# Padded loads, a reordered opening, GpSimd triangles and unit-matrix products in a chunked linear-attention kernel with a feed-forward block

## The chip, the cores and the metric

The kernel runs on one core of one Trainium2 chip. The metric is device time in microseconds (us) of the whole program. Before the change the median of three timed runs is 633.68 us (632.99 to 636.66).

## The reference

Two stages, in float32. A recurrent attention over 768 steps with a state of 40 x 40 for each of 4 batches and 8 heads (32 independent systems), and then a feed-forward block on its output, with 320 channels (8 heads of 40) and 1280 hidden ones.

```python
# B, H, S, D = 4, 8, 768, 40
for t in range(S):
    kt, vt, rt = (k[:, :, t], v[:, :, t], r[:, :, t])
    wt, at, bt = (w[:, :, t], a[:, :, t], b[:, :, t])
    y[:, :, t] = np.einsum('bhd,bhde->bhe', rt, state)
    Sa = np.einsum('bhde,bhe->bhd', state, at)
    state_decay = state * wt[:, :, None, :] - np.einsum('bhd,bhe->bhde', Sa, bt)
    state = state_decay + np.einsum('bhd,bhe->bhde', vt, kt)
...
x = y.transpose(0, 2, 1, 3).reshape(B, S, H * D)
xn = (x - mu) / np.sqrt(var + 1e-06) * g_ln
out = x + np.maximum(xn @ w_ch1, 0.0) @ w_ch2
```

The inputs arrive as host arrays that were laid out beforehand: `ea` holds w and a of a chunk, `eb` k and b, `rd` and `vr` r and v by rows of the 40 channels, `vt` v by steps. The two weight matrices arrive as float64 and are turned into float32 on the chip.

## The kernel before, in words

**Chunks.** The 768 steps are cut into 24 chunks of 32, and the recurrence inside a chunk is solved in closed form with products of small matrices; two chunks make a slab. The 32 systems lie in two halves of 16, one at partition rows 0 to 39, one at 64 to 103, so a tile of "104 rows" holds both.

**One chunk** passes these steps, each a function of the code.

- `prep` loads `wa` (from `ea`) and `bk` (from `eb`). VectorE forms running products of w with scans: `gE` (L335), its reciprocal `last` (L337), and `qE` backwards (L339). `aT` = a * qE (L343) and `bk` *= gE (L351), on VectorE for chunks below `EARLY` = 4 and on GpSimd from there. A transfer puts aT into the block tile `abd`. TensorE forms the gram products (L361, bank<-abd,bk), VectorE evacuates them with a mask of signs into `gk` (L364), and transfers store gk to DRAM (`d_l`, the triangles; `d_k`, the part for the products with x).
- `invert`, once a slab: the triangles of both chunks come back from DRAM into `yv` (64 partitions, one system of one chunk each), and 14 steps of two VectorE instructions (L403 into ytmp, L407 into yv) invert their diagonal blocks; a ScalarE copy (L409) and two stores (`d_h`) follow.
- `merge`: four loads of `hv` from d_h, two TensorE products (L428, L439) and two ScalarE copies (`qm`, `tt`) make the full inverse of a chunk.
- `loads`: transfers into the operand tiles (`x2s`, `x5s`, `vu`), and transposes of bk by TensorE (L464).
- `chain` is the recurrence proper: the product L487, its negated copy `hn` (ScalarE), the product with the inverse (L497, bank<-hn,tt), four ScalarE copies into x (L501), the state update (L514) and its VectorE evacuation with the decay (L521).
- `post` makes the output of a chunk: transposes of u (L535) and of the state (ScalarE copies behind them), `rbd` loaded from `rd`, a product `z` masked into `x5s` by VectorE (L573), the product y and its evacuation `xt` (L588).
- `norm` and `moe`: layer norm of xt and its transposes; for every two chunks ten blocks of the hidden layer, each with eight up products (L753), ScalarE `hh`, VectorE `hl` (L758, the low part of a two-part split) and six down products (L737).

**The weights.** `weights` loads them after the mark ("go",), which is chunk 0's qE scan, and converts them in 22 quarters through three buffers (`ot_0`, `ot_1`, `m`). A quarter is: ScalarE Abs, VectorE's shift (L626) and merge of the low word (L627), then the sign. For some quarters the sign is VectorE's third pass (L630); for ten quarters of w2 (`sel`) ScalarE makes a Sign and GpSimd multiplies by it (L634). Behind it stand the scaling and the high copy, and a residue `w` = m - high on GpSimd (L670), after which the buffer is free.

**The order.** All of this is entered as tasks into a planner (`Plan`) with an engine, an estimated duration, a key (a due time in chunks) and what the task reads and writes. `Plan.order` is a list scheduler: it gives each engine the ready task that can start first and, among those, the one of the lowest key, with its estimates alone. The result is one fixed row of instructions for TensorE, VectorE, ScalarE, GpSimd and for SyncE, which issues all transfers in order. For a transfer the planner assumes kb/200 us on the pipe. ("first",) marks the task behind which the transfers of chunks 2 and 3 may go.

Of the kernel before, what the change touches and what calls it, by code (L numbers as in the profile page):

```python
# [11 lines left out]
F32 = mybir.dt.float32  # L12
# [8 lines left out]
NCH = 24  # L21
# [11 lines left out]
ROWS = [slice(r, r + D) for r in HROW]  # L33
QUADS = [slice(32 * q, 32 * q + 32) for q in range(4)]
SLAB = 2
NSLAB = NCH // SLAB
EARLY = 4
# [12 lines left out]
class Plan:  # L50
# [4 lines left out]
    READ, FETCH, STALL = 128, 3.6, 0.2  # L55

# [28 lines left out]
    def order(self, free):  # L85
# [31 lines left out]
        while len(out) < len(T):  # L117
# [41 lines left out]
            if t["eng"] == "SP":  # L159
                pipe = max(pipe, end + 1.3) + t["kb"] / 200.0  # L160
                done = pipe + 0.7 + t["late"]
# [13 lines left out]
        return out  # L175


@with_exitstack
def body(ctx, tc, ea, eb, vr, rd, vt, w1, w1x_in, w2, gl, fe, fd, out):
# [35 lines left out]
    gk, = ring(1, "gk", 512)  # L215
# [31 lines left out]
    two = lambda x, i, n=2: [(x, i, y) for y in range(n)]  # L247

# [72 lines left out]
    def prep(c):  # L321
        i, s, j, k = c % 2, c // SLAB, c % SLAB, c % BK
        kp = c - 3.4
# [3 lines left out]
        after = [("first",)] if 2 <= c < 4 else []  # L327
        kl = kp + (0.5 if 2 <= c < 4 else -1.0 if c < 2 else 0.0)
        for hf in (1, 0):
            dma(kl - 1.3, 167, after, [W[hf]], t[ROWS[hf]], ea[c, hf])  # L330
        for hf in (1, 0):
            dma(kl - 1.1, 164, after, [K[hf]], tb[ROWS[hf]], eb[c, hf])
        R = slice(0, 104)
        n = 528
        op("DVE", 1.25, kp, W + ["start0"], [("g", i)], lambda: nc.vector.tensor_tensor_scan(  # L335
            out=flat(g[R]), data0=t[R, 0:n], data1=flat(start0[R]), initial=0.0, op0=ALU.mult, op1=ALU.max))
        op("DVE", 0.24, kp, [("g", i)], ["last"], lambda: nc.vector.reciprocal(  # L337
            out=last[R, :, C:33], in_=g[R, :, C:33]))
        op("DVE", 1.25, kp, W + ["last"], [("q", i)] + ([("go",)] if c == 0 else []), lambda: nc.vector.tensor_tensor_scan(  # L339
            out=flat(q[R])[:, ::-1], data0=t[R, n:0:-1], data1=flat(last[R])[:, ::-1], initial=0.0,  # L340
            op0=ALU.mult, op1=ALU.max))
        eng, e, us = ("DVE", nc.vector, 1.0) if c < EARLY else ("POOL", nc.gpsimd, 1.8)
        op(eng, 0.7 * us, kp, W + [("q", i)], A + ([("first",)] if c == 1 else []), lambda: e.tensor_tensor(  # L343
            out=at[R, 0:512].rearrange("p (h t) -> p h t", t=C),
            in0=t[R, 529:1041].rearrange("p (h t) -> p h t", h=16), in1=q[R, :, 1:33], op=ALU.mult))
        for hf, rs in enumerate(ROWS):
            dma(kp + 0.05, 82, A, [("abd", 0, hf)], abd[rs, hf].rearrange("p h t -> p (h t)"), at[rs, 0:512])
        op("ACT", 0.25, kp, [("g", i)], [("pc", c % AT)], lambda: nc.scalar.copy(
            out=at[R, 512:528], in_=g[R, :, C:33].rearrange("p h o -> p (h o)")))
        kb = tb[R].rearrange("p (h x t) -> p h x t", h=16, x=2)  # L350
# [125 lines left out]


    def chain(c):
        i, o = c % 2, (c + 1) % 2
        b = Bank("A")  # L480

        def f(b=b):
# [472 lines left out]
```

## Time and profile before

| | us |
|---|---|
| timed runs: median, lowest, highest | 633.68, 632.99, 636.66 |
| profiled execution, its own time | 636.37 |
| its span | 634.6 |
| TensorE products busy | 537.4 (85%) |
| VectorE busy | 446.5 (70%) |
| ScalarE busy | 323.6 (51%) |
| GpSimd busy | 117.6 (19%) |
| mean busy share of the 16 DMA engines | 48.8% |

The profile is that of one execution, and its times are counted from the start of the span. A row of a group reads: line, engine, operation, out<-in, shapes, count, then busy us in all, mean ns of one, and the idle time ahead of it with what ended it. A row in order of time reads: start, duration, engine, line, and in brackets the wait ahead of it and what ended it. TensorE's shares are means over stages: they are low in the opening, where the weights are converted and the first slab is made, and high behind it.

### The profile page before, as it was taken

To read this page: it belongs to the slowest core of one execution; us is meant where nothing else is said; L and a number is where in the kernel's file an instruction comes from. 1 tells how busy PE (TensorE), PEld (TensorE's weight loads), DVE (VectorE), ACT (ScalarE), POOL (GpSimd) and SP (SyncE) were. 2 spreads that over 40 slices of the span, in tenths; PEclk is the share of its full clock that TensorE was granted. 3 is DMA by queue.
4 is the path that set the end of the run, shared out by engine and by line. 5 is a ranking of instruction groups with operands and counts; after the bars stand their busy time and mean duration, and the time that the engine had idled before them with its cause. 6 is when DMAs were issued, how large, how long until landed. Compare 5 with 4: busy or idle time off the path is not lost.

```text
span 634.6 us, 35137 instructions
## 1 busy us (share of the span) xinstructions
PE 537.4 (85%) x15610; PEld 489.7 (77%) x15610; DVE 446.5 (70%) x1114; ACT 323.6 (51%) x836; POOL 117.6 (19%) x109
## 2 busy tenths in 40 slices
PE   0714875888959989899989999999789899999995
PEld 0514764777858879889989988888779799888995
DVE  7588699996488695595785885864876845967742
ACT  9726756664434454564455355354256545644421
POOL 9108055612021220120221021021022100000000
PEclk9999975798969999999989999799799999999998
DMA  6666667365654554446556356446445445452200
GB/s 170 160 176 171 158 161 206 78 155 121 158 152 125 139 134 106 127 122 156 141 127 163 92 138 151 102 112 159 108 122 143 113 106 119 117 134 79 88 32 25
DMA packets 132205, 81.63 MB, mean 129 GB/s; under 512 B 102736, under 2 KB 108880, under 8 KB 132048
## 3 DMA queue, kind: packets, MB, share of 16 engines
q1 hardware_dynamic: 132048, 79.32, 48.8%
q8 instruction: 124, 2.03, 1.3%
q14 instruction: 33, 0.27, 0.2%
HBM read 51.64 MB, written 12.58 MB: 101 GB/s over the span
## 4 chain that ended last, share of the span: by engine, by line
PE 57%; DVE 16%; issue 8%; SPq 6%; DMA 6%; ACT 4%; POOL 2%; DVEq 0%; ACTq 0%; POOLq 0%
PE bank L737 15%; PE bank L753 13%; SPq L253 6%; PE bank L514 4%; PE bank L567 4%; DVE ytmp L403 3%; DVE yv L407 3%; PE bank L361 3%; PE bank L550 3%; PE bank L584 2%; PE bank L464 2%; PE bank L487 2%; PE bank L439 2%; PE bank L535 2%; PE bank L497 2%
## 5 line engine op out<-in xcount | busy, mean ns | idle before, releaser
L737 PE MATMUL bank<-w,hh 128*128 128x320 f32 x480 | 120.2, 336 | 0.0
L753 PE MATMUL bank<-xh,w 128*128 128x256 f32 x480 | 109.2, 289 | 2.2 <-DVE hl L758 1.7
L756 ACT ACTIVATE hh<-bank 128x256 fp32r<-128x256 f32 x120 | 46.1, 384 | 125.3 <-PE bank L753 123.1
L758 DVE SCALAR_TENSOR_TENSOR hl<-bank,hh 128x256 fp32r<-128x256 f32 x120 | 50.3, 420 | 68.3 <-ACT hh L756 65.6
L753 PEld LDWEIGHTS bank<-xh,w 128*128 128x128 f32 x480 | 83.8, 192 | 3.4 <-DVE hl L758 2.0
L351 POOL TENSOR_TENSOR bk<-bk,gE 104x1024 f32<-104x1024 f32 x20 | 45.9, 2294 | 217.5 <-DMA bk<-in_eb_dram 140.3
L737 PEld LDWEIGHTS bank<-w,hh 128*128 128x128 f32 x480 | 79.7, 196 | 3.8
L737 PE MATMUL bank<-w,hl 128*128 128x320 f32 x240 | 76.1, 317 | 0.1
L753 PE MATMUL bank<-xl,w 128*128 128x256 f32 x240 | 68.4, 285 | 1.2 <-DVE xl L725 1.2
L361 PE MATMUL bank<-abd,bk 104*64 104x64 f32 x768 | 32.1, 245 | 35.8 <-POOL mask L266 14.7
L403 DVE TENSOR_TENSOR ytmp<-yv 64x28 f32<-64x28 f32 (+6 forms) x168 | 43.2, 257 | 23.3 <-issue 11.1
L469 ACT COPY xk<-bank 64x320 f32<-64x320 f32 x96 | 40.2, 418 | 35.3 <-PE bank L464 30.9
L361 PEld LDWEIGHTS bank<-abd,bk 104*64 104x64 f32 x768 | 28.8, 157 | 38.0 <-POOL mask L266 14.6
L521 DVE TENSOR_TENSOR x<-bank,x2s 40x320 f32<-40x320 f32 x92 | 44.6, 485 | 10.6 <-PE bank L514 8.4
L514 PE MATMUL bank<-x,xk 128*40 128x40 f32 (+1 forms) x1472 | 43.1, 220 | 9.2 <-ACT x L501 6.1
L514 PEld LDWEIGHTS bank<-x,xk 128*40 128x40 f32 (+1 forms) x1472 | 36.8, 133 | 15.4 <-ACT x L501 6.8
L553 ACT COPY xk<-bank 40x320 f32<-40x320 f32 x96 | 40.2, 418 | 15.2 <-PE bank L550 13.8
L407 DVE TENSOR_TENSOR yv<-yv,ytmp 64x28 f32<-64x28 f32 (+6 forms) x168 | 43.5, 259 | 5.8
L737 PEld LDWEIGHTS bank<-w,hl 128*128 128x128 f32 x240 | 46.9, 195 | 0.7 <-DVE hl L758 0.6
L753 PEld LDWEIGHTS bank<-xl,w 128*128 128x128 f32 x240 | 46.2, 193 | 1.5 <-DVE xl L725 1.5
L573 DVE TENSOR_TENSOR x5s<-bank,mask 64x256 f32<-64x256 f32 x96 | 40.5, 422 | 9.0 <-PE bank L567 6.7
L335 DVE TENSOR_TENSOR_SCAN gE<-wa,start 104x528 f32<-104x528 f32 x24 | 30.8, 1283 | 20.8 <-DMA wa<-in_ea_dram 11.8
(122 smaller groups left out, 1046.5 us busy)
## 6 DMA issues: line engine op xcount, KB each, us to landing
wa<-in_ea_dram SPq DMA_DIRECT2D x48, 162.7 KB
bk<-in_eb_dram SPq DMA_DIRECT2D x48, 160.0 KB
xk<-xk SPq DMA_DIRECT2D x48, 160.0 KB
x2s<-aT SPq DMA_DIRECT2D x48, 82.5 KB
wa<-in_ea_dram SPq DMA_DIRECT2D x24, 165.0 KB
rbd<-in_rd_dram SPq DMA_DIRECT2D x48, 80.0 KB
x<-in_vt_dram SPq DMA_DIRECT2D x48, 80.0 KB
abd<-aT SPq DMA_DIRECT2D x48, 80.0 KB
```

The costliest lines, as they stand in the source:

```text
L351: op(eng, 1.25 * us, kp, [("g", i)], K, lambda: e.tensor_tensor(out=kb, in0=kb, in1=g[R, :, 0:C].unsqueeze(2).broadcast_to([104, 16, 2, C] ...
L361: mm(pg[64 * bb:64 * bb + 64, :, h], lhsT=tb[R, 64 * p:64 * p + 64], rhs=abd[R, :, p], start=True, stop=True)
L403: nc.vector.tensor_tensor(out=tv, in0=yb[:, :, j + 1:, j:j + 1].broadcast_to(S), in1=yb[:, :, j:j + 1, 0:j].broadcast_to(S), op=ALU.mult)
L407: nc.vector.tensor_tensor(out=v, in0=v, in1=tv, op=ALU.add)
L469: op("ACT", 0.45, c - 1.2 + 0.1 * bb, [bs[hf]], [X[hf]], lambda b=bs[hf], zs=zs, hf=hf, bb=bb: nc.scalar.copy(out=xk[i][zs, 1, hf, 8 * bb: ...
L514: mm(pst[ROWS[hf], h], lhsT=xk[i][FROW[hf], 1, hf, p], rhs=x2[i][FROW[hf], hf, p], start=True, stop=True)
L521: nc.vector.tensor_tensor(out=x2[o][rs, hf, ps], in0=bank[b.at][rs, 0:CH].rearrange("p (h e) -> p h e", e=D), in1=x2s[o][rs, hf, 512 + 8 * ...
L573: op("DVE", 0.4, c + 0.5, [b, "mask"], [("z", i)], lambda b=b, zs=zs, ps=ps, hf=hf, bb=bb: nc.vector.tensor_tensor(out=x5s[i][zs, hf, 8 * ...
L737: mm(bank_of(po[u])[:, 0:CH], lhsT=l[:, us], rhs=ws[f"w2_{f}"][:, x], start=f == 0 and n == 0, stop=f == 9 and n == 2)
L753: mm(ph, lhsT=l, rhs=r, start=n == 0, stop=n == 7)
L756: yield "ACT", 0.39, [phs[f]], [("hh", f % 2)], lambda f=f: nc.scalar.activation(out=hht[f % 2], in_=bank_of(phs[f])[:, 0:256], func=AF.Re ...
L758: yield "DVE", 0.42, [phs[f], ("hh", f % 2)], [("hl", f % 2)], lambda f=f: nc.vector.scalar_tensor_tensor(out=hlt[f % 2], in0=bank_of(phs[ ...
```

## The change

What it does, part by part:

1. The loads of 40 rows a half (`ea`, `eb`, `rd`, `vr`, and aT into abd and x2s) become loads of 48: the host arrays are padded (with 1 for w, else 0), and the scans and the products of `prep` run on 112 rows.
2. Chunks 0 and 1: abd is written by VectorE in two half products, and the transfer of aT into abd is gone; aT comes from it by two ScalarE copies. Chunk 1 takes `rbd` for abd and `aT[2]` for gk, so that it does not wait for chunk 0's. `EARLY` is 2: chunks 2 and 3 form aT and bk on GpSimd.
3. `soon` lowers the keys of chunks 0 and 1 by two. ("first",) is now the evacuation of chunk 1's gram products, and releases chunk 2's transfers as well as chunk 0's and 1's qc and transposes of bk; ("second",), the last step of the first slab's triangles, releases chunk 3's transfers.
4. The triangles are inverted by GpSimd, except those of the first slab.
5. The signs: all quarters take VectorE's third pass, the three passes are three tasks, and Sign and GpSimd's product are gone.
6. `Plan.fill` puts products of the unit matrix (`warm`, 128 x 256, into bank 7, which nothing reads before it is written anew) into the gaps that the planner sees on TensorE from 10 us up to the first up product; there are 51.
7. The planner's pace for transfers is kb/240 in place of kb/200, and the check of w at the end reads 96 rows in place of 80.

```diff
+DP = 48
+LROWS = [slice(r, r + DP) for r in HROW]
-EARLY = 4
+EARLY = 2
...
+    FILL = 0.7
...
-                pipe = max(pipe, end + 1.3) + t["kb"] / 200.0
+                pipe = max(pipe, end + 1.3) + t["kb"] / 240.0
...
+    def fill(self, out, since, us, fn):
+
+        res, at = [], since
+        for t in out:
+            if t["eng"] == "PE":
+                if t["dense"]:
+                    at = 1e9
+                for _ in range(int((t["start"] - at) * self.FILL / us)):
+                    res.append(dict(start=at, n=-1, us=us, eng="PE", fn=fn))
+                    at += us / self.FILL
+                at = max(at, t["start"] + t["us"])
+        return sorted(out + res, key=lambda t: (t["start"], t["n"]))
...
+    soon = lambda c: 2.0 if c < SLAB else 0.0
...
-        kp = c - 3.4
+        kp = c - 3.4 - soon(c)
...
-        after = [("first",)] if 2 <= c < 4 else []
+        after = [("first",)] if c == 2 else [("second",)] if c == 3 else []
+        ab, an = (rbd, "rbd") if c == 1 else (abd, "abd")
+        gk, gn = (aT[2][:, 0:512], ("aT", 2)) if c == 1 else (gk1, "gk")
...
-            dma(kl - 1.3, 167, after, [W[hf]], t[ROWS[hf]], ea[c, hf])
+            dma(kl - 1.3, 200, after, [W[hf]], t[LROWS[hf]], ea[c, hf], queue=low)
...
-        R = slice(0, 104)
+        LR = slice(0, 112)
...
+        if c < 2:
+            for hf, rs in enumerate(LROWS):
+                op("DVE", 0.7, kp, W + [("q", i)], [(an, 0, hf)], lambda hf=hf, rs=rs: nc.vector.tensor_tensor(
+                    out=ab[rs, hf], in0=t[rs, 529:1041].rearrange("p (h t) -> p h t", h=16), in1=q[rs, :, 1:33],
+                    op=ALU.mult))
+                op("ACT", 0.65, kp + 1.0, [(an, 0, hf)], A, lambda hf=hf, rs=rs: nc.scalar.copy(
+                    out=at[rs, 0:512].rearrange("p (h t) -> p h t", t=C), in_=ab[rs, hf]))
+        else:
+            op(eng, 0.7 * us, kp, W + [("q", i)], A, lambda: e.tensor_tensor(
...
+            for hf, rs in enumerate(LROWS):
+                dma(kp + 0.05, 98, A, [("abd", 0, hf)], abd[rs, hf].rearrange("p h t -> p (h t)"), at[rs, 0:512])
...
-        op("DVE", 0.68, kp + 0.3, [b, "sign"], ["gk"], lambda b=b: nc.vector.tensor_tensor(
+        op("DVE", 0.68, kp + 0.3, [b, "sign"], [gn] + ([("first",)] if c == 1 else []), lambda b=b: nc.vector.tensor_tensor(
...
+        go = [("first",)] if c < 2 else []
...
     def invert(s):
-        k0 = c0 - 2.0
+        eng, e, us = ("DVE", nc.vector, 0.54) if s == 0 else ("POOL", nc.gpsimd, 0.75)
+        k0 = c0 - 2.0 - 2 * soon(c0)
...
-                nc.vector.tensor_tensor(
+                e.tensor_tensor(
...
-                nc.vector.tensor_tensor(out=v, in0=v, in1=tv, op=ALU.add)
-            op("DVE", 0.6, k0 + 0.02 * j, (), ["y", "ytmp"], f)
+                e.tensor_tensor(out=v, in0=v, in1=tv, op=ALU.add)
+            op(eng, us, k0 + 0.02 * j, (), ["y", "ytmp"] + ([("second",)] if s == 0 and j == B - 2 else []), f)
...
     def merge(c):
-        km = c - 0.55
+        km = c - 0.55 - soon(c)
...
     def chain(c):
+        k = c - soon(c)
...
     def conv(i, key):
-                if sel:
-                    nc.scalar.activation(out=hi.bitcast(F32), in_=hi.bitcast(F32), func=AF.Sign)
-            op("ACT", 0.95 if sel else 0.45, key, [res], [("ot", mi)] + sg, f)
+            op("ACT", 0.45, key, [res], [("ot", mi)], f)
...
-            if sel:
-                op("POOL", 0.9, key, [res] + sg, [("ot", mi)], lambda: nc.gpsimd.tensor_tensor(
-                    out=m.bitcast(F32), in0=m.bitcast(F32), in1=hi.bitcast(F32), op=ALU.mult))
+            V = nc.vector
+            for n, f in enumerate((
+                    lambda: V.tensor_scalar(out=m, in0=m, scalar1=3, scalar2=None, op0=ALU.logical_shift_left),
+                    lambda: V.scalar_tensor_tensor(
+                        out=m, in0=lo, scalar=29, in1=m, op0=ALU.logical_shift_right, op1=ALU.bitwise_or),
+                    lambda: V.scalar_tensor_tensor(
+                        out=m, in0=hi, scalar=0x80000000, in1=m, op0=ALU.bitwise_and, op1=ALU.bitwise_or))):
+                op("DVE", 0.5 if n else 0.35, key, [res], [("ot", mi)], f)
...
-        for t in P.order(dict(A=[0, 1, 2, 3], H=[4, 5], M=[6, 7])):
+        def warm():
+            mm(bank[7][:, 0:256], lhsT=ident, rhs=ident.unsqueeze(1).broadcast_to([128, 2, 128]), start=True, stop=True)
+        for t in P.fill(P.order(dict(A=[0, 1, 2, 3], H=[4, 5], M=[6, 7])), 10.0, 0.45, warm):
             t["fn"]()
...
-    def rows(x):
-        return x.reshape(NCH, 2, 16, C, D).transpose(0, 1, 4, 2, 3)
+    def rows(x, pad=0):
+        y = np.full((NCH, 2, DP, 16, C), pad, np.float32)
+        y[:, :, :D] = x.reshape(NCH, 2, 16, C, D).transpose(0, 1, 4, 2, 3)
+        return y
```

Where the diff moves instructions, the engines' fixed rows show it. The line numbers of the new kernel differ from those of the old one; names end in a number that tells buffers apart.

VectorE in the opening, from chunk 0's aT on. gE, last and qE are the scans and their reciprocal, gk the evacuation of the gram products. Before:

```order
L343 TENSOR_TENSOR aT_82<-wa_73,qE_80 104x512
L351 TENSOR_TENSOR bk_75<-bk_75,gE_78 104x1024
L335 SCALAR_TENSOR_TENSOR gE_79<-wa_74,start_0_71 104x528
L337 RECIPROCAL last_72<-gE_79 104x16
L339 SCALAR_TENSOR_TENSOR qE_81<-wa_74,last_72 104x528
L343 TENSOR_TENSOR aT_83<-wa_74,qE_81 104x512
L351 TENSOR_TENSOR bk_76<-bk_76,gE_79 104x1024
L364 TENSOR_TENSOR gk_87<-bank_144,sign_70 128x512
L335 SCALAR_TENSOR_TENSOR gE_78<-wa_73,start_0_71 104x528
L364 TENSOR_TENSOR gk_87<-bank_146,sign_70 128x512
```

And now:

```order
L367 TENSOR_TENSOR abd_85<-wa_73,qE_80 48x512 x2
L381 TENSOR_TENSOR bk_75<-bk_75,gE_78 112x1024
L357 SCALAR_TENSOR_TENSOR gE_79<-wa_74,start_0_71 112x528
L359 RECIPROCAL last_72<-gE_79 112x16
L396 TENSOR_TENSOR gk_87<-bank_144,sign_70 128x512
L361 SCALAR_TENSOR_TENSOR qE_81<-wa_74,last_72 112x528
L367 TENSOR_TENSOR rbd_86<-wa_74,qE_81 48x512 x2
L381 TENSOR_TENSOR bk_76<-bk_76,gE_79 112x1024
L396 TENSOR_TENSOR aT_84<-bank_147,sign_70 128x512
L357 SCALAR_TENSOR_TENSOR gE_78<-wa_73,start_0_71 112x528
```

The half products stand where aT stood; chunk 0's evacuation moved from behind chunk 1's products to the middle of chunk 1's scans, and chunk 1's evacuation (into aT_84, which serves as its gk) now stands ahead of chunk 2's first scan.

GpSimd around the second slab's triangles: w are the residues of the weights (L670 before, L700 now), yv and ytmp the triangles. Before:

```order
L670 TENSOR_TENSOR w_0_852<-ot_142,w_0_852 128x320
L343 TENSOR_TENSOR aT_83<-wa_73,qE_80 104x512
L670 TENSOR_TENSOR w_0_1_858<-ot_141,w_0_1_858 128x256
L670 TENSOR_TENSOR w_1_1_962<-ot_142,w_1_1_962 128x256
L634 TENSOR_TENSOR m_143<-m_143,r_2_207 128x320
L634 TENSOR_TENSOR ot_141<-ot_141,r_3_208 128x320
L670 TENSOR_TENSOR w_2_1305<-m_143,w_2_1305 128x320
```

And now, where the last two rows are the first of 14 such pairs:

```order
L700 TENSOR_TENSOR w_1_861<-m_143,w_1_861 128x320
L373 TENSOR_TENSOR aT_83<-wa_73,qE_80 112x512
L700 TENSOR_TENSOR w_0_949<-ot_142,w_0_949 128x320
L429 MEMSET yv_89 64x32
L437 TENSOR_TENSOR ytmp_90<-yv_89 64x28
L441 TENSOR_TENSOR yv_89<-yv_89,ytmp_90 64x2x14
```

The 28 instructions of the triangles came into GpSimd's row between residues; three residues (w_0_1, w_1_1, w_2) stand behind them. The two sign products are gone.

TensorE between the gram products and the first product with the inverse: 361/393 gram, 428/462 and 439/473 the merge, 497/533 the product with the inverse, 850 the products of the unit matrix. Before:

```order
L361 MATMUL bank_145<-abd_85,bk_77 64x2x32 x16
L379 MATMUL bank_144<-ident,qc_88 128x104 x4
L361 MATMUL bank_146<-abd_85,bk_75 64x2x32 x16
L428 MATMUL bank_147<-hv_91 32x16 x32
L439 MATMUL bank_145<-hv_91,qm_93 32x32 x32
L428 MATMUL bank_144<-hv_92 32x16 x32
L497 MATMUL bank_146<-hn_106,tt_94 32x40 x32
```

And now:

```order
L393 MATMUL bank_146<-abd_85,bk_77 64x2x32 x16
L850 MATMUL bank_151<-ident 128x256 x15
L462 MATMUL bank_144<-hv_91 32x16 x32
L850 MATMUL bank_151<-ident 128x256
L473 MATMUL bank_147<-hv_91,qm_93 32x32 x32
L462 MATMUL bank_145<-hv_92 32x16 x32
L533 MATMUL bank_146<-hn_106,tt_94 32x40 x32
L850 MATMUL bank_151<-ident 128x256 x3
```

Only one gram product (chunk 2's) is left between the first slab's and the merge, chunk 3's moved behind, and 15 products of the unit matrix stand ahead of the merge, one within it and three behind.

123 lines of the change are left out of this document (57 added, 66 removed).

## The prediction

> **What bounds the kernel now.** I read the stages first: busy time of each engine before and after 119 us, where the last conversion of the weights leaves VectorE (columns: stretch, length, busy us and count on PE, PEld, DVE, ACT, POOL, granted clock, DMA share, GB/s).
>
> ```profile
> 0.00:119.00 119.00, 62.83 (x1782) 54.72 (x1784) 94.91 (x191) 79.34 (x189) 54.81 (x72) 0.87 0.62 163
> 119.00:635.00 516.00, 474.56 (x13834) 435.02 (x13830) 351.59 (x924) 244.21 (x647) 62.74 (x38) 0.96 0.48 121
> ```
>
> There are two regimes. After 119 us TensorE is busy 92% and everything else waits for it. Before, TensorE is busy for half of the time and VectorE for 80%. The profiled execution took 636.4 us with a span of 634.6; the median of the three timed runs is 633.7, so I make the sum against 636.4 and take off 2.7 at the end.
>
> The waits of TensorE after 119 us come next (engine and line, releaser: us in all, times, longest).
>
> ```profile
> PE bank L535 <- issue: 5.7, 4, 2.0
> PE bank L514 <- ACT x L501: 5.5, 2, 4.8
> ...
> PE bank L361 <- DVE x L521: 2.9, 1, 2.9
> PE bank L753 <- DVE hl L758: 1.7, 1, 1.7
> ```
>
> The "issue" waits have no releaser and stay. The other three, 10 us, are waits on ScalarE and VectorE, and are what a lighter VectorE can touch.
>
> Last, the opening, in order of time.
>
> ```profile
> 6.18 1.26 DVE L335 TENSOR_TENSOR_SCAN gE<-wa,start 104x528 f32<-104x528 f32 x1 [1.70 <-DMA wa<-in_ea_dram]
> ...
> 14.67 1.98 PE L361 MATMUL bank<-abd,bk 104*64 104x64 f32 x32 [14.67 <-POOL mask L266]
> ...
> 23.18 1.97 PE L361 MATMUL bank<-abd,bk 104*64 104x64 f32 x32
> ...
> 25.26 0.69 DVE L364 TENSOR_TENSOR gk<-bank,sign 128x512 f32<-128x512 f32 x1 [0.52 <-PE bank L361]
> ...
> 32.06 0.53 SPq L253 DMA_DIRECT2D yv<-d_l  x1
> ...
> 36.93 0.09 DVE L395 MEMSET yv<- 64x32 f32 x1
> ...
> 44.42 0.64 ACT L409 COPY yv<-yv 64x256 f32<-64x256 f32 x1 [8.03 <-DVE yv L407]
> ...
> 59.00 1.27 PE L497 MATMUL bank<-hn,tt 32*32 32x40 f32 x64
> ...
> 85.05 1.15 PE L361 MATMUL bank<-abd,bk 104*64 104x64 f32 x32 [0.94 <-DMA abd<-aT]
> ...
> 118.91 0.42 DVE L573 TENSOR_TENSOR x5s<-bank,mask 64x256 f32<-64x256 f32 x1
> ```
>
> This is the path of the first slab: first scan at 6.2 us, products of chunk 0 (14.7) and chunk 1 (23.2), their evacuation (25.3), the reload of the triangles (32.1), the triangles on VectorE (36.9 to 44.4), the first product with the inverse (59.0). Its last row, chunk 2's x5s behind the last conversion, is my milestone: in both orders it stands at the same point of the work.
>
> **The first two chunks.** The gram product of chunk 0 stands until 14.7 us because its abd arrives by a transfer from aT; the page names the mask, which is not its operand. Without the transfer it needs only bk. With the first scan at 6.2, VectorE's two scans of 1.26, the reciprocal, two half products and the bk product follow:
>
> ```profile
> L343 DVE TENSOR_TENSOR aT<-wa,qE 104x512 f32<-104x512 f32 x4 | 2.8, 692 | 0.1
> ...
> L351 DVE TENSOR_TENSOR bk<-bk,gE 104x1024 f32<-104x1024 f32 x4 | 4.9, 1220 | 0.0
> ```
>
> 6.2 + 1.26 + 0.3 + 1.26 + 2 x 0.69 + 1.22 = 11.6 us, 3 earlier. Chunk 1 needs another 0.69 (evacuation of chunk 0) + 1.26 + 0.3 + 1.26 + 1.38 + 1.22 = 6.1: 17.7 instead of 23.2, and evacuation at about 20 instead of 25.3. On SP the way to the reload is not free. ScalarE now makes aT (four copies of half width, about 0.65 each, behind its constants), and the r load into rbd waits for that copy and for chunk 1's product ahead of chunk 1's d_l stores. I put the stores at 21.5 and the reload at 25, 7 earlier. Chunk 2's loads now wait for the evacuation and stand just ahead of the reload, so the data comes at 28 to 29 and the triangles start at about 30.
>
> **Loads of 48 rows.** Two stretches show the spread of rows over DMA engines (same columns as the stages).
>
> ```profile
> 3.00:5.00 2.00, 0.00 (x0) 0.00 (x0) 1.19 (x5) 1.99 (x4) 1.62 (x8) 1.00 0.63 163
> ...
> 60.00:66.00 6.00, 3.51 (x169) 3.16 (x162) 2.50 (x4) 4.58 (x12) 3.17 (x4) 1.00 0.94 262
> ```
>
> While loads of 40 rows run alone, the share is 0.63, ten engines of sixteen; with other shapes in flight it reaches 0.94 and 262 GB/s. Bytes rise by a fifth. If 48 rows spread over all sixteen, the 4.5 us to the first scan become 4.5 x 1.2 x 163 / 262 = 3.4, a gain of 1; if they stay on ten, a loss of 0.9. I take 0.5 of gain. Later transfers lie beside other work.
>
> **Conversion of the weights and the lock.** In the sum of VectorE up to the milestone the change takes out one slab's 28 triangle instructions (0.26 each by the row further down: 7.4 us) and the aT and bk products of chunks 2 and 3 (2 x 1.9 = 3.8). It adds a third pass in ten quarters (10 x 0.49), two extra half products (1.4), and 3.5 of chunk work that the new order puts ahead. Net -1.4. What the passes really cost depends on GpSimd:
>
> ```profile
> L627 DVE SCALAR_TENSOR_TENSOR ot<-r,ot 128x320 uint32<-128x320 uint32 x6 | 6.6, 1094 | 0.2
> ...
> L627 DVE SCALAR_TENSOR_TENSOR ot<-rx,ot 128x320 uint32<-128x320 uint32 x2 | 1.0, 491 | 0.1
> ...
> L634 POOL TENSOR_TENSOR m<-m,r 128x320 f32<-128x320 f32 x4 | 4.5, 1134 | 12.8 <-issue 12.8
> ```
>
> ```profile
> 46.36 1.86 POOL L659 TENSOR_TENSOR w1x<-ot,w1x 64x320 fp32r<-64x320 f32 x2 [28.43 <-issue]
> 46.37 1.12 DVE L630 SCALAR_TENSOR_TENSOR m<-r,m 128x256 uint32<-128x256 uint32 x1
> ```
>
> The same pass takes 491 ns with GpSimd silent and 1094 beside it; the second pair shows one held up inside a GpSimd product. This speaks against the triangles on GpSimd. The Trainium skill, page "SBUF — State Buffer", section "Who interferes with whom", says that a VectorE instruction with two SBUF inputs and a GpSimd instruction that reads SBUF exclude each other for the whole instruction; the trace agrees (1.12 us for a 256-wide pass). By that rule alone 28 more GpSimd instructions per slab would hold VectorE for up to their whole length, about 11 us a slab, and the gain below would be gone. I do not take that end: only the scans (four a slab) and a few small instructions have two SBUF inputs after 119 us, the rest read PSUM. In the opening the ten sign products (about 1 us each) leave GpSimd, while 28 triangles and two chunks' products (2 x 3.5) enter. Of the 12.6 us by which the 94.9 exceed counts times undisturbed rows, I keep 10: -2.5.
>
> **The path to the milestone.** Triangles from 30, held up by GpSimd's products for chunk 2 (3.5 us), end near 39 to 41 instead of 44.4. Between them and the first product with the inverse lie 14.6 us now (store, reload, merges, with ScalarE's conversions ahead of a merge's copy). The order keeps most of that; 12 leaves 52 instead of 59: -7. VectorE's idle time (119 - 94.9 = 24.1) falls by as much. So -7 - 1.4 - 2.5, about -11: milestone near 108. Ends: 98, if idle time falls to 14 and locks to 6; 119, if the second slab's triangles, which now stand on GpSimd ahead of the residues w of three weights, stop the conversions, whose three buffers they free.
>
> **Fill products.** 51 products of 256 columns stand ahead of waiting ones.
>
> ```profile
> 20.00:30.00 10.00, 8.31 (x168) 6.83 (x168) 5.72 (x7) 7.92 (x21) 0.00 (x0) 1.00 0.66 170
> ```
>
> TensorE was busy 8.3 of 10 us here, and yet the gram product ran 1.97 us at 23.2; only the one at 85.1 ran 1.15. The Trainium skill, page "TensorE: Matmul & The Clock Gate", Part 1, has the clock double after about 3.4 us of sustained activity and fall back after an idle window; the printed clock of 1.00 at 20 to 30 us does not agree with the durations, so durations decide. By the rule the fills would raise the clock from about 25 us on. The eight products between the merge and chunk 1's z, 1.1 to 2 us each, would save 4 to 5 us if they all ran as at 85 us; if fills come late by a few products, they cost 0.4 each. I take -1, inside the 12 above. Their cover is the wait for the triangles; with triangles early by 4 us, up to 4 us of it would show.
>
> **TensorE at the milestone.** In the new order these products already stand ahead of chunk 2's z: three more half transposes of bk, and of chunk 3 one merge, one x2s product and one with the inverse, and half of a state update (rows of the chain, at full clock).
>
> ```profile
> 128.32 0.41 PE bank L464 x16
> ...
> 130.75 0.73 PE bank L487 x62
> ...
> 132.95 0.72 PE bank L497 x64
> ```
>
> 3 x 0.41 + 4 x 0.7 = 4 us of work that is behind TensorE when it becomes the bound: -4.
>
> **Triangles on GpSimd after 119 us.** What VectorE pays now, and GpSimd's nearest rows:
>
> ```profile
> 119.00:635.00 516.00, 73.53 (x280) 0.96 0.48 121
> ```
>
> ```profile
> L351 POOL TENSOR_TENSOR bk<-bk,gE 104x1024 f32<-104x1024 f32 x17 | 38.2, 2250 | 217.5 <-DMA bk<-in_eb_dram 140.3 <-DMA hv<-d_h 26.4 <-PE bank L720 20.1
> L343 POOL TENSOR_TENSOR aT<-wa,qE 104x512 f32<-104x512 f32 x18 | 22.3, 1238 | 105.4 <-DVE qE L339 52.3 <-DMA x2s<-aT 15.7 <-DMA x2s<-d_k 14.8
> ```
>
> ```profile
> L659 POOL TENSOR_TENSOR w1x<-ot,w1x 64x320 fp32r<-64x320 f32 x4 | 3.6, 891 | 28.7 <-issue 28.4
> ...
> L267 POOL TENSOR_SCALAR_AFFINE_SELECT sign<-sign 32x32 f32<-32x32 f32 x4 | 0.8, 207 | 0.3
> ```
>
> From 512 to 1024 elements 1.01 us, so 2 ns an element and 0.23 fixed. The triangles have 28 to 112 elements, 80 in the mean: 0.39 us, bounded by 0.21 (a 32-element select) and 0.89 (the smallest product). 28 of them with pauses of 0.04 take 12 us. On VectorE they are 7.4 us of work, but interleaved:
>
> ```profile
> 489.35 0.09 DVE L395 MEMSET yv<- 64x32 f32 x1
> ...
> 499.44 0.68 ACT L409 COPY yv<-yv 64x256 f32<-64x256 f32 x1 [0.29 <-DVE yv L407]
> ...
> 504.04 2.86 SPq L253 DMA_DIRECT2D hv<-d_h  x4
> ...
> 513.22 0.81 PE L428 MATMUL bank<-hv 32*32 32x16 f32 x64
> ```
>
> 10.1 us from first to last, so GpSimd is only 2 us later. Reload issue and transfer end near 509, the merge starts at 513: 4 us to spare. VectorE loses 73.5 of 351.6 us. Of TensorE's 10 us of waits on it and ScalarE, and of the half-clock stretches behind them (0.96 of 516 us), I take 6: -6. Ends: -18, and +4 if locks delay the evacuations.
>
> **Sum.** -11 - 4 - 6 = -21, with the 0.5 of the loads -21.5: 636.4 becomes 615, and 612 on the scale of the median.
>
> **The rivals.** Late triangles, the side of slower: spare time is 10.1 + 4, so 14.1 us for 28 instructions; above 0.5 us each (with pauses) the merge waits in every slab, ten times. From 0.56 us on this eats the 15 us of the other terms; at 0.65 it is (28 x 0.65 - 14.1) x 10 = 41 us, 633.7 - 15 + 41 = 660. For it: the smallest product measured is 0.89. Against it: that one has 320 elements, and the slope is clean. 11%.
>
> Opening unchanged: the conversions wait for GpSimd's triangles, the milestone stays at 115 to 119, and 4 + 6 remain, less 1 to 4: 624 to 630. For it: GpSimd sits on the reload ahead of the residues. Against it: ten sign products are gone. 20%.
>
> More than forecast: milestone at 98 to 100 and 10 to 15 us of waits and half-clock gone after it: 593 to 602. 13%.
>
> The change does not do what it says: 48 rows stay on ten engines and fills never raise the clock. That takes away 0.5 + 0.9 of the loads and 1 of the fills and leaves 614, inside the forecast.
>
> **Numbers.** Forecast (603 to 623) 56%, at 612. Within 1% is 627.4 to 640.0, about what a measurement can tell from no change. Faster by over 1%: 0.56 + 0.13 + half of 0.20 = 0.79, less 0.02 for waits behind hv in some slabs alone: 0.77. Within 1%: the other half of 0.20, that 0.02 and 0.01 of the late triangles: 0.13. Slower: 0.10. The range of 8 in 10 leaves out the late triangles and the far end of the better case: 597 to 631.
>
> **What would show it.** Chunk 0's gram product at about 11 us and chunk 1's at 18; DMA share near 1 in the first 5 us; triangles on GpSimd at 0.3 to 0.45 us each; gram products of 1.1 us before 50 us; the first product with the inverse at about 52; chunk 2's x5s at 100 to 113; fewer than 6 us of TensorE waiting on ScalarE and VectorE after it. It is wrong if GpSimd's triangles pass 0.5 us, if TensorE waits for hv in several slabs, or if the last conversion ends after 115.

## The result and the profile after

The changed kernel takes 689.08 us in the median (687.67 to 692.32) beside 634.66 for the kernel before: a ratio of 1.0863, interval 1.081 to 1.0917. It is slower by about 54 us; I had forecast 612. The profiled execution has a span of 688.1 us. Ratios here and below compare the fast runs alone, so they need not be the quotient of two medians.

First the stages, cut at the same point of the work as before: behind the last conversion of the weights, which is at 131 us in place of 119 (columns as in the prediction).

```profile
0.00:131.00 131.00, 87.63 (x2165) 72.71 (x2166) 100.77 (x177) 79.89 (x194) 64.72 (x98) 0.80 0.73 168
131.00:688.00 557.00, 490.16 (x13556) 449.23 (x13552) 275.73 (x627) 238.02 (x638) 164.82 (x325) 0.92 0.51 121
```

The opening lost 12 us and the rest 41. In the rest VectorE's busy time fell from 351.6 to 275.7 us, as forecast, and the time did not follow: TensorE, 92% busy before, is 88% busy. Its idle time rose from 41.4 (516 - 474.6) to 66.8 us, and about as many products (13556 records, 13834 before) took 15.6 us more, at a granted clock of 0.92 in place of 0.96.

The waits of TensorE behind 131 us, in the form of those shown before:

```profile
PE bank L473 <- ACT qm L464: 9.0, 2, 6.9
PE bank L462 <- DMA hv<-d_h: 6.6, 6, 3.7
PE bank L587 <- ACT xk L590: 6.5, 2, 6.3
PE bank L533 <- ACT hn L526: 5.1, 5, 2.6
...
PE bank L393 <- POOL ytmp L437: 3.2, 1, 3.2
```

The first three were not among those of before. Lines 462 and 473 are the merge, but only the 6.6 us at line 462 are a wait for the inverted triangles. The longest waits at 473 (6.9) and 587 (6.3) end just after a stand of ScalarE at its small copy into aT, which waits until a transfer from the same buffer into x2s has landed:

```profile
299.32 0.22 ACT L378 COPY aT<-gE 112x16 f32<-112x16 f32 x1 [7.84 <-DMA x2s<-aT]
...
353.90 0.22 ACT L378 COPY aT<-gE 112x16 f32<-112x16 f32 x1 [9.83 <-DMA x2s<-aT]
```

In all ScalarE waits there for 56.1 us, beside 18.4 in the kernel before (us in all, times, longest; the kernel before second):

```profile
ACT aT L378 <- DMA x2s<-aT: 56.1, 16, 9.8
```

```profile
ACT aT L348 <- DMA x2s<-aT: 18.4, 9, 3.2
```

The opening in order of time (start, duration, engine, line):

```profile
12.23 1.98 PE L393 MATMUL bank<-abd,bk 104*64 104x64 f32 x32 [12.23 <-DMA x<-in_vt_dram]
14.14 4.80 PE L850 MATMUL bank<-ident 128*128 128x256 f32 x12
...
19.27 1.15 PE L393 MATMUL bank<-rbd,bk 104*64 104x64 f32 x32
...
29.89 0.51 SPq L271 DMA_DIRECT2D yv<-d_l  x1
...
32.67 1.26 DVE L357 TENSOR_TENSOR_SCAN gE<-wa,start 112x528 f32<-112x528 f32 x1 [11.51 <-DMA wa<-in_ea_dram]
...
35.55 0.09 DVE L429 MEMSET yv<- 64x32 f32 x1
...
36.80 2.18 POOL L381 TENSOR_TENSOR bk<-bk,gE 112x1024 f32<-112x1024 f32 x1
...
36.94 2.11 DVE L437 TENSOR_TENSOR ytmp<-yv 64x52 f32<-64x52 f32 x1
...
45.91 0.63 ACT L443 COPY yv<-yv 64x256 f32<-64x256 f32 x1 [8.52 <-DVE yv L441]
...
58.98 1.29 PE L533 MATMUL bank<-hn,tt 32*32 32x40 f32 x64 [1.01 <-ACT tt L475]
...
77.80 0.49 SPq L271 DMA_DIRECT2D yv<-d_l  x1
...
129.86 1.05 DVE L663 SCALAR_TENSOR_TENSOR ot<-r,ot 128x320 uint32<-128x320 uint32 x1
```

The gram products came about as forecast, at 12.2 and 19.3 us. Then the lead melts. VectorE's row has chunk 2's scans ahead of the first triangles, and stands idle for 11.5 us until that chunk's data is there; the triangles begin at 35.6 and one of their products of about 0.2 us takes 2.11 beside GpSimd's 2.18. The Trainium skill, "SBUF — State Buffer", section "Who interferes with whom", has such a pair exclude each other for the whole instruction; these two rows agree with it. The triangles end at 45.9 (44.4 before), the first product with the inverse stands at 59.0 as before, and the second slab's reload comes at 77.8. The row for that reload in the kernel before:

```profile
60.30 0.50 SPq L253 DMA_DIRECT2D yv<-d_l  x1
```

### The profile page after: what moved, and what is told of

It reads as the page before. It is cut to its first block, busy times and chain, and to the rows that moved or that the text cites. A ratio compares the mean times of both kernels' runs of the same rounds, so it can differ in the third digit from the quotient of the medians.

```text
span 688.1 us, 35325 instructions
## 1 busy us (share of the span) xinstructions
PE 577.8 (84%) x15714; PEld 521.9 (76%) x15714; DVE 376.5 (55%) x803; ACT 317.9 (46%) x830; POOL 229.5 (33%) x422
## 4 chain that ended last, share of the span: by engine, by line
PE 41%; DMA 14%; POOL 14%; SPq 10%; DVE 8%; issue 8%; ACT 4%; DVEq 0%; POOLq 0%; ACTq 0%
SPq L271 10%; PE bank L783 10%; PE bank L767 9%; POOL ytmp L437 6%; POOL yv L441 6%; DMA wa<-in_ea_dram 3%; DMA yv<-d_l 3%; PE bank L393 3%; PE bank L550 2%; PE bank L604 2%; PE bank L572 2%; DMA hv<-d_h 2%; PE bank L621 2%; PE bank L587 2%; PE bank L523 1%
## 5 line engine op out<-in xcount | busy, mean ns | idle before, releaser
L767 PE MATMUL bank<-w,hh 128*128 128x320 f32 x480 | 123.3, 343 | 0.0
L783 PE MATMUL bank<-xh,w 128*128 128x256 f32 x480 | 115.1, 300 | 0.6 <-ACT xh L754 0.6
L381 POOL TENSOR_TENSOR bk<-bk,gE 112x1024 f32<-112x1024 f32 x22 | 51.5, 2343 | 166.1 <-DMA bk<-in_eb_dram 143.8
L783 PEld LDWEIGHTS bank<-xh,w 128*128 128x128 f32 x480 | 89.2, 205 | 1.5 <-ACT xh L754 0.8
L357 DVE TENSOR_TENSOR_SCAN gE<-wa,start 112x528 f32<-112x528 f32 x24 | 31.7, 1325 | 71.1 <-DMA wa<-in_ea_dram 46.9
L441 POOL TENSOR_TENSOR yv<-yv,ytmp 64x28 f32<-64x28 f32 (+6 forms) x154 | 58.8, 382 | 12.1
L437 POOL TENSOR_TENSOR ytmp<-yv 64x28 f32<-64x28 f32 (+6 forms) x154 | 56.1, 365 | 11.2
L504 ACT COPY xk<-bank 64x320 f32<-64x320 f32 x96 | 40.1, 418 | 32.7 <-PE bank L499 31.1
L373 POOL TENSOR_TENSOR aT<-wa,qE 112x512 f32<-112x512 f32 x22 | 26.1, 1185 | 84.0 <-DMA x2s<-aT 44.2
L783 PEld LDWEIGHTS bank<-xl,w 128*128 128x128 f32 x240 | 49.3, 205 | 0.4 <-DVE xl L755 0.4
L610 DVE TENSOR_TENSOR x5s<-bank,mask 64x256 f32<-64x256 f32 x96 | 40.5, 422 | 14.6 <-PE bank L604 10.6
L393 PE MATMUL bank<-abd,bk 104*64 104x64 f32 x736 | 30.8, 245 | 15.7 <-DMA x<-in_vt_dram 12.2
L537 ACT COPY x<-bank 32x320 f32<-32x320 f32 x96 | 40.0, 416 | 7.6 <-PE bank L533 5.9
```

The lines of the kernel that those rows point to most:

```text
L381: op(eng, 1.25 * us, kp, [("g", i)], K, lambda: e.tensor_tensor(out=kb, in0=kb, in1=g[LR, :, 0:C].unsqueeze(2).broadcast_to([112, 16, 2, C ...
L393: mm(pg[64 * bb:64 * bb + 64, :, h], lhsT=tb[R, 64 * p:64 * p + 64], rhs=ab[R, :, p], start=True, stop=True)
L437: e.tensor_tensor(out=tv, in0=yb[:, :, j + 1:, j:j + 1].broadcast_to(S), in1=yb[:, :, j:j + 1, 0:j].broadcast_to(S), op=ALU.mult)
L441: e.tensor_tensor(out=v, in0=v, in1=tv, op=ALU.add)
L610: op("DVE", 0.4, k + 0.5, [b, "mask"], [("z", i)], lambda b=b, zs=zs, ps=ps, hf=hf, bb=bb: nc.vector.tensor_tensor(out=x5s[i][zs, hf, 8 * ...
L767: mm(bank_of(po[u])[:, 0:CH], lhsT=l[:, us], rhs=ws[f"w2_{f}"][:, x], start=f == 0 and n == 0, stop=f == 9 and n == 2)
```

## The experiments

They ran in five batches, not all on one chip. In each batch the kernel before ran beside them on the same chip, at 641.8 to 644.6 us in the median; so I give ratios with their intervals. The changed kernel was not run again in them: its ratio is the 1.0863 from above. Names beginning with a are the changed kernel with something undone, those with b the kernel before with something done. Theories: G, the triangles on GpSimd; L, the longer loads; P, the order that the planner makes, in the opening and by its faster pace.

**Undone or done one at a time.** a_tri_dve:

```diff
-        eng, e, us = ("DVE", nc.vector, 0.54) if s == 0 else ("POOL", nc.gpsimd, 0.75)
+        eng, e, us = "DVE", nc.vector, 0.54
```

> The changed kernel with all triangles on VectorE again; the planner makes its own order for it. Theory G (triangles on GpSimd hold back the products for the next chunks in GpSimd's row and the merges behind them, about 4 us in each of 11 slabs): the time falls by 35 to 50 us, to 640 to 655. Theory L (48-row loads make the transfers late): it falls by under 10 us, to 680 or more. Theory P (the order that the planner makes, in the opening and with its faster pace for transfers): 670 to 690.

Measured 1.0682 (1.0555 to 1.0809), 678.0 us. a_40:

```diff
-DP = 48
+DP = 40
...
-        LR = slice(0, 112)
+        LR = slice(0, 104)
```

> The changed kernel with loads of 40 rows again and the order of instructions unchanged. Theory L: the time falls by 25 us or more, to under 665. Theories G and P: within 8 us of 689.

Measured 1.0681 (1.0612 to 1.075). b_tri_pool puts only the triangles on GpSimd, b_48 pads only the loads (one of them is shown; the products of `prep` run on 112 rows as in the change):

```diff
+        eng, e, us = ("DVE", nc.vector, 0.6) if s == 0 else ("POOL", nc.gpsimd, 0.75)
...
-            op("DVE", 0.6, k0 + 0.02 * j, (), ["y", "ytmp"], f)
+            op(eng, us, k0 + 0.02 * j, (), ["y", "ytmp"], f)
```

```diff
-            dma(kl - 1.3, 167, after, [W[hf]], t[ROWS[hf]], ea[c, hf])
+            dma(kl - 1.3, 167, after, [W[hf]], t[LROWS[hf]], ea[c, hf])
```

> The kernel before with the triangles of all slabs but the first on GpSimd (0.75 us a pair for the planner, as in the change), nothing else. Theory G: 665 to 685. Theories L and P: 625 to 645.

Measured 1.0351 (1.0236 to 1.0467).

> The kernel before with loads of 48 rows, same order of instructions. Theory L: 655 or more. Theories G and P: 630 to 642.

Measured 1.0313 (1.0215 to 1.0411). No single theory holds: a_tri_dve came out where P had it, b_48 where L had it, the other two where none did. Each of the two parts alone costs about 3%, and undoing either gives back about 2 of 8.6%. I had priced both as gains.

**The rest.** a_40_tri undoes both.

> The changed kernel with 40-row loads and all triangles on VectorE. If the two prices add (each undone alone gave about 1.8%), the ratio to the kernel before is 1.05, about 667 us, and a third part of the change has a price of its own of 5%. If the two hold back the same chain, so that undoing both frees it, the ratio is 1.00 to 1.02, 634 to 647 us.

Measured 1.0375 (1.0245 to 1.0505), between the two cases: a third part remains. b_240:

```diff
-                pipe = max(pipe, end + 1.3) + t["kb"] / 200.0
+                pipe = max(pipe, end + 1.3) + t["kb"] / 240.0
```

> The kernel before with the planner's faster pace for transfers (240 in place of 200) alone: the same work in another order. If the order made by 240 is itself the third part: ratio 1.03 or more, 653 us or more. If not: within 1% of the kernel before. Either way it shows how much a newly planned order moves the time.

Measured 1.0183 (1.0053 to 1.0313): the same work in another order costs 1.8% (0.5 to 3.1). b_fill adds `fill` and `warm` alone, b_conv the new `conv` alone, b_conv_fill both, each as the diff of the change has them.

> The kernel before with the products of the unit matrix alone (70 of them in its own order, which is otherwise unchanged). If they raise the clock in the opening and do nothing else: first clock record near 20 us in place of 83.7, 628 to 634 us. If they use up what the clock has later (more half-clock stretches after 155 us than the 37.5 us of before) or stand in the way of the first slab: 640 us or more.

Measured 1.0033 (0.9969 to 1.0097): no difference that can be told.

> The kernel before with the signs by VectorE in every quarter of the weights and the passes as three tasks, nothing else. If VectorE bounds the opening: ten more passes of 0.49 us, less what GpSimd's ten products no longer hold up, 632 to 640 us. If the new tasks let other work of VectorE in between and the buffers come free later: 645 us or more.

Measured 0.9907 (0.9864 to 0.9949): the one part that gains.

> The kernel before with the signs by VectorE and the products of the unit matrix together: the signs alone gave 0.991, the products alone 1.003. If they add: 0.994, 630 to 640 us. If the clock that the products raise is worth something once the conversions are shorter: 0.985 or less.

Measured 1.0012 (0.9971 to 1.0054). Beside the fills the signs' gain is gone; the intervals of b_conv and b_conv_fill, from two batches, do not overlap.

a_200 gives the changed kernel the old pace (the edit of b_240 backwards), a_open also 40-row loads with their old sizes in the plan and triangles on VectorE.

> The changed kernel with the planner's old pace for transfers (200) and nothing else. If the pace is a part of the loss in the changed kernel as it is alone (1.8%): ratio to the kernel before about 1.067, 678 us. If the pace only matters beside 40-row loads (240 and a fifth more bytes cancel in the plan): 1.08 to 1.09, 686 to 693 us.

Measured 1.0667 (1.0603 to 1.0732): the pace costs 2% here too. The plan of the change counts 200 KB / 240 for a load that was 167 / 200 before: 0.83 us by either. It takes the longer load for as long as the shorter one was.

> The changed kernel with 40-row loads, triangles on VectorE and the planner's old pace and sizes: what is left of the change is the opening (keys, half products, aT by ScalarE, the marks first and second), the signs and the products of the unit matrix. If the opening has no price of its own: 0.99 to 1.00 of the kernel before, 629 to 640 us. If its order costs: 1.02 or more, 647 us or more.

Measured 1.0247 (1.0168 to 1.0327): what is left, the opening, the signs and the fills in their new order, has a price of its own.

**Why the triangles cost.** b_tri_swap keeps the order of the kernel before and changes only the engine of the 28 instructions; b_tri_long leaves them on VectorE and makes seven of them twice (first the edit of the one, then of the other):

```diff
+        e = nc.vector if s == 0 else nc.gpsimd
...
-                nc.vector.tensor_tensor(
+                e.tensor_tensor(
```


```diff
+                if s and j % 2:
+                    nc.vector.tensor_tensor(
+                        out=tv, in0=yb[:, :, j + 1:, j:j + 1].broadcast_to(S),
+                        in1=yb[:, :, j:j + 1, 0:j].broadcast_to(S), op=ALU.mult)
```

> The kernel before with its order of instructions kept, but the triangles of all slabs but the first run by GpSimd at the places that the plan gave them on VectorE. If the execution on GpSimd holds the merges and the next chunks' products back: ratio 1.025 or more, 650 us or more. If only the order that the planner makes for GpSimd is bad: within 1% of the kernel before.

Measured 1.0189 (1.0129 to 1.0249), between the two cases of the expectation.

> The kernel before with every second product of the triangles done twice on VectorE in all slabs but the first (seven more instructions, about 2 us a slab), same order. If the triangles' length is on the path that sets the end: 10 to 22 us more, ratio 1.015 to 1.035, like the triangles run by GpSimd at the same places (1.0189). If it is not the length but what waits behind them in GpSimd's row: under 1.008.

Measured 1.0261 (1.0166 to 1.0357), as for a length that counts. But the seven instructions also give VectorE more to do (365.8 us behind 119 us in place of 351.6), and this run does not part the two. In b_tri_swap VectorE has less to do and the kernel is slower all the same: what the two runs share is the longer row of triangles. A slab of b_tri_swap, GpSimd's row in order of time:

```profile
407.32 0.15 POOL L396 MEMSET yv<- 64x32 f32 x1
...
411.19 1.18 POOL L343 TENSOR_TENSOR aT<-wa,qE 104x512 f32<-104x512 f32 x1
412.34 0.40 POOL L404 TENSOR_TENSOR ytmp<-yv 64x108 f32<-64x108 f32 x1
...
416.58 1.25 POOL L408 TENSOR_TENSOR yv<-yv,ytmp 64x100 f32<-64x100 f32 x1
...
420.57 0.23 POOL L408 TENSOR_TENSOR yv<-yv,ytmp 64x28 f32<-64x28 f32 x1
```

From the first row to ScalarE's copy it takes 13.5 us, with another product of the row between and single instructions held up (1.25 in place of about 0.4 us). The time from the memset to ScalarE's copy, mean of the ten slabs behind 119 us of each profile, against the loss:

| kernel | triangles, us a slab | ratio |
|---|---|---|
| before | 10.6 | 1 |
| b_tri_long | 12.2 | 1.0261 |
| b_tri_swap | 13.1 | 1.0189 |
| after | 12.7 | 1.0863 (all parts) |

1.6 us more in each of eleven slabs is 17 us, and 2.6% is 17 us (11 to 23 by the interval), VectorE's added work included; 2.5 us more is 27 us, of which 12 came through. So the 4 us of spare time that I counted on did not cover even these 1.6 and 2.5 us.

The merge, where I had looked for spare time, is not where they came through. These are waits behind 119 us in the kernel before, in b_tri_long and in b_tri_swap (there ScalarE's and TensorE's):

```profile
ACT yv L409 <- DVE yv L407: 12.9, 6, 4.0
```

```profile
ACT yv L413 <- DVE yv L411: 21.8, 9, 4.5
```

```profile
ACT yv L410 <- POOL yv L408: 41.8, 10, 8.2
...
PE bank L515 <- ACT x L502: 9.5, 2, 9.0
...
PE bank L429 <- DMA hv<-d_h: 0.2, 1, 0.2
```

TensorE waits for the inverted triangles (hv) for 0.2 us in all of b_tri_swap. But ScalarE, whose row is fixed, stands at its copy of the triangles, and the copies for the recurrence (x, hn, xk) stand behind it. TensorE's waits of over 0.4 us that fall into these stands add up to 5.8 us in the kernel before, 12.1 in b_tri_long and 13.2 in b_tri_swap, where the rise is about 7 of the 12 us lost. SyncE stands in the same way at the store of the triangles (d_h<-yv), with all later transfers behind it: 2.2, 8.4 and 19.6 us in ten slabs, and 25.7 in the changed kernel. What SyncE's stands cost is not shown.

In the changed kernel TensorE's waits within ScalarE's stands at the triangles are only 3.3 us. There the copy into aT (line 378) holds ScalarE up more: 56.1 us, 50.4 with loads of 40 rows (a_40), but 22.3 with the triangles on VectorE (a_tri_dve). It goes with an order that is made for triangles on GpSimd: b_tri_pool has 32.5, b_tri_swap, which keeps the old order, 20.4. What in such an order does it is not shown.

**Why the loads cost.** Two stretches of b_48, the first with the loads alone, and the DMA queue of both kernels (packets, MB, share of 16 engines; the kernel before first):

```profile
3.00:5.00 2.00, 0.00 (x0) 0.00 (x0) 1.19 (x5) 1.99 (x4) 1.62 (x8) 1.00 1.03 194
...
119.00:640.00 521.00, 471.27 (x13783) 430.60 (x13783) 348.49 (x915) 244.45 (x645) 65.60 (x40) 0.95 0.57 131
```

```profile
q1 hardware_dynamic: 132048, 79.32, 48.8%
```

```profile
q1 hardware_dynamic: 142896, 87.27, 57.3%
```

The rows do spread: the share goes from 0.63 to 1.03. But the rate goes only from 163 to 194 GB/s (172 in the changed kernel) for a fifth more bytes, so the load is no earlier, and over the whole span the queue is busy longer (10% more bytes, 57.3 in place of 48.8%; behind 119 us a share of 0.57 for 131 GB/s, beside 0.48 for 121). Which wait carries this to the end is not shown. The first scan of the changed kernel is not earlier than before (6.18) either:

```profile
6.53 1.26 DVE L357 TENSOR_TENSOR_SCAN gE<-wa,start 112x528 f32<-112x528 f32 x1 [2.04 <-DMA wa<-in_ea_dram]
```

b_48_plan tells the planner the sizes, at the old pace.

> The kernel before with 48-row loads and the planner told of their size, at the old pace. If b_48 lost (1.0313) because the plan took the transfers for shorter than they are: 1.00 to 1.01. If the bytes themselves cost: 1.02 or more.

Measured 1.0123 (1.003 to 1.0217). The intervals just touch: it looks as if some two thirds of the 3.1% in b_48 were an order made for shorter loads, and 1.2% stayed with an order that knows them; but that order is a new one, and b_240 shows what a new one alone can do.

**What in the opening costs.** Three more, built on a_open or on the kernel before. a_first:

```diff
-        after = [("first",)] if c == 2 else [("second",)] if c == 3 else []
+        after = [("first",)] if 2 <= c < 4 else []
```

> The kernel a_open (the changed one with 40-row loads, triangles on VectorE, the old pace) with one word changed: chunk 3's loads wait for the mark first, as before, and not for second, the end of the first triangles. If the late loads of chunk 3 are what makes the second slab and the opening late: the product with the inverse of chunk 2 comes 8 us or more earlier than at 115.2 us, and the ratio falls from 1.0247 to 1.00 to 1.01. If the half products, the keys or the unit products are at fault: 1.02 or more.

Measured 1.0224 (1.0139 to 1.0309): no better. The product with the inverse of chunk 2 came at 111.7 in place of 115.2 us, which is a part of the shift, but the conversions ended at 130.4 as in a_open (131.3). VectorE's passes over the weights were long there, and GpSimd's four products of chunks 2 and 3 were the suspects. b_early2 and a_early4 differ from the kernel before and from a_first in the number at `EARLY`.

> The kernel before with EARLY = 2 alone: the four products of chunks 2 and 3 (aT and bk) by GpSimd. If GpSimd's products hold VectorE's passes over SBUF up in the opening: the last conversion stays at 118 to 122 us although VectorE has 3.8 us less to do, the passes are longer in the mean, ratio 1.00 to 1.015. If moving them relieves VectorE: 0.99 or less.

Measured 0.993 (0.9863 to 0.9997), between the two cases; the median of all its ten runs is 643.1 us beside 644.6, so I count it as no difference.

> The kernel a_first (the changed opening with 40-row loads, triangles on VectorE, old pace, chunk 3 behind the mark first) with EARLY = 4 again. If GpSimd's four products are what makes the conversions late: the last conversion comes at 125 us or earlier in place of 130.4, and the ratio falls from 1.0224 to under 1.012. If the keys and the half products are at fault: 1.018 or more.

Measured 1.0222 (1.0139 to 1.0305). The two passes over `ot` up to 130 us in a_first, and then in a_early4 (count | busy us, mean ns):

```profile
L663 DVE SCALAR_TENSOR_TENSOR ot<-r,ot 128x256 uint32<-128x256 uint32 (+1 forms) x13 | 10.3, 789 | 0.4
L661 DVE SCALAR_TENSOR_TENSOR ot<-r,ot 128x256 uint32<-128x256 uint32 (+1 forms) x13 | 10.0, 771 | 0.4
```

```profile
L661 DVE SCALAR_TENSOR_TENSOR ot<-r,ot 128x256 uint32<-128x256 uint32 (+1 forms) x12 | 7.0, 581 | 0.4
L663 DVE SCALAR_TENSOR_TENSOR ot<-r,ot 128x256 uint32<-128x256 uint32 (+1 forms) x12 | 7.0, 580 | 0.4
```

The passes are shorter by about a quarter, and the time is the same: this theory falls. In a_early4 the last conversion came at 132.5 us, behind two of VectorE's waits, for the loads and for ScalarE's Abs (us in all, times, longest), which are longer than in the kernel before (second):

```profile
DVE gE L357 <- DMA wa<-in_ea_dram: 13.3, 2, 11.3
DVE ot L660 <- ACT ot L654: 6.4, 2, 5.2
```

```profile
DVE gE L335 <- DMA wa<-in_ea_dram: 7.9, 3, 6.0
...
DVE ot L626 <- ACT ot L619: 2.0, 2, 1.3
```

What is left for the 2.2% are the keys, the half products, the mark first, which now stands behind chunk 1's evacuation, and the newly made order as such, which cost 1.8% in b_240; none was tried alone, and this stays open.

**A version that beats both.** b_conv_e6 is b_conv with four more products taken off GpSimd in the opening:

```diff
-EARLY = 4
+EARLY = 6
```

> A version that may beat both: the kernel before with the signs by VectorE (0.991 alone) and EARLY = 6, which takes four more products off GpSimd in the opening. If they hold VectorE up for more than the 3.8 us that they cost there: 0.985 or less. If not: 0.99 to 1.00.

Measured 0.984 (0.9766 to 0.9914): faster than the kernel before by 1.6%. Its lead over b_conv, 0.7%, is within the intervals of the two.

## Why the prediction was wrong, point by point

Taken from the kernel before to the changed one, the ratios climb in four steps, each difference good to 1 to 1.5%, and all but the last with a newly made order: opening, signs and fills 1.0247 (a_open); pace and sizes of the plan 1.0375 (a_40_tri); triangles 1.0681 (a_40); loads 1.0863. That is 2.5, 1.3, 3.1 and 1.8%, or 16, 8, 19 and 12 us; the 1.3% alone could not be told from nothing.

- **Triangles: the step that failed is the spare time.** The durations were right, and the rows show it (columns: count | busy us, mean ns):

```profile
L441 POOL TENSOR_TENSOR yv<-yv,ytmp 64x28 f32<-64x28 f32 (+6 forms) x154 | 58.8, 382 | 12.1
L437 POOL TENSOR_TENSOR ytmp<-yv 64x28 f32<-64x28 f32 (+6 forms) x154 | 56.1, 365 | 11.2
```

  Forecast 0.39 us each and 12 us a slab; measured 0.37 and 12.7. "GpSimd is only 2 us later" held, but "4 us to spare" came from one slab, and from one place in it: the time between the landing of the inverted triangles (near 509 us) and their merge (513). The rows that stop earlier, ScalarE's at the copy and SyncE's at the store, I did not look at. In b_tri_swap 2.5 us more a slab cost 12 us while the merge waited for 0.2. The rival of the late triangles had the right part and the wrong wait and threshold: at 0.37 us each, under its 0.5, the merge waits 6.6 us in six slabs, and most of the loss lies elsewhere. In place of the 6 us of TensorE's waits that were to go, its idle time behind the milestone rose by 25 us, at a lower granted clock; the loads and the new order have their part in that.
- **Loads: "Later transfers lie beside other work" failed.** I weighed 0.5 us of gain against 0.9 of loss for the first load alone. They cost 1.8% with all else changed and 3.1% alone, though the spread over the engines that I had hoped for took place. The stretch with 262 GB/s from which I took the rate held other shapes; loads of this shape reached 194 with all engines busy.
- **The planner's pace had no term in the sum.** I took the order as given and priced its instructions. b_240 and a_200 put 1.8 and 2% on it, each good to about a percent.
- **The path to the milestone: the reload and what stands ahead of the triangles failed.** The gram products came within 1.6 us of the forecast, the reload at 29.9 in place of 25, the triangles at 35.6 in place of 30, and the first product with the inverse at 59.0 in place of 52, no earlier than before. I had chunk 2's data at 28 to 29 us, and it came at 32.7; and I had not counted that its scans stand ahead of the triangles in VectorE's row, another 2.9 us. The milestone came at 131, outside my ends of 98 to 119. VectorE's busy time ahead of it, forecast to fall by 1.4 and 2.5 us, rose from 94.9 to 100.8, and its idle time, forecast to fall by 7 from 24.1, rose to 30.2. The rival of the opening did happen in part: GpSimd waits 11.6 us for the second slab's triangles, and no residue passes from 71.5 to 95.8 us. But a_open, with those triangles on VectorE, ends its conversions no earlier (131.3).
- **Signs.** I had ten passes of 0.49 us as a cost and the silence of GpSimd as a relief. Together, tried on the kernel before, they gain: b_conv is 0.9% faster, about 6 us. Which of its three edits (the sign on VectorE, no product on GpSimd, passes as separate tasks) does it was not tried.
- **Fills.** They did what I said to the gram product: 1.98 us at 12.2, 1.15 at 19.3, with 4.8 us of fills between. That agrees with the Trainium skill, "TensorE: Matmul & The Clock Gate", Part 1 (a higher clock after about 3.4 us of sustained work). No gain came of it that can be told: b_fill 1.0033 (0.9969 to 1.0097).
- **The 4 us of products that stand ahead of the milestone** were not tried alone, and no run shows what they were worth.

## What to carry to other kernels

Free time on an engine says nothing about a chain. Before moving a step to a slower engine, look at every fixed row in which something stands for its result, the copies and stores as well as the product that uses it, and try the step on the new engine with the order kept. A static order is a part of the kernel like any instruction: when a change touches the durations in the planner, price the new order by itself, and keep its sizes and pace at what the transfers measure. Padding a load so that it spreads over more DMA engines is worth something only if the rate rises by more than the bytes; here it did not.

## What the runs showed that I had not expected

In the stretch from 3 to 5 us sixteen busy DMA engines moved 48-row loads at 172 to 194 GB/s where ten moved 40-row loads at 163. And planning anew moved this kernel by 1.8% in the one case where nothing else was changed (b_240), as much as most of the parts did, so a single variant that is planned anew says little about a part of 1%: b_tri_swap and b_48, which keep the order, can be read more directly than b_tri_pool.
